# The lower part of w_out's rounded weights: half of it made on GpSimd in two of every four steps

## The chip, the core and the metric
The kernel runs on one core of one Trainium2 chip. The metric is the device time of one execution in microseconds, as the median of several runs. The core has five engines that matter here: TensorE (PE, with its weight loads shown as PEld), VectorE (DVE), ScalarE (ACT), GpSimd (POOL) and SyncE (SP), which issues the transfers.

## The reference
The kernel computes a linear attention with decay and feeds the result to a two-layer network.

```
for each block b of 64 positions:
    intra = (q_b k_b^T * decay mask) v_b
    inter = (q_b * lam^(pos+1)) kv_state
    out[b] = intra + inter
    kv_state = lam^64 * kv_state + (k_b * lam^(63-pos))^T v_b
x = out as 3072 tokens x 512 features
h = x @ w_in                  # 512 x 2048
y = relu(h)^2 @ w_out         # 2048 x 512
```

Everything is float32. There are 4 batches, 8 heads, 768 positions and 64 features in a head.

## The kernel before
**Tokens and slices.** The 3072 tokens make 24 chunks of 128. Four chunks are one slice of 512 tokens, so there are six slices. In a slice the network runs over 16 blocks `f` of 128 hidden features. For each block, `hidden(m, f)` makes h with 12 matmuls, ScalarE and VectorE make relu(h)^2, and `project(m, f)` adds its product with w_out to four PSUM banks (`acc`) with 12 matmuls. The diff touches slice 1 alone, which the code calls m = 0.

**Two parts to each number.** A float32 value is kept as an upper part of few bits and a lower part that holds what is left. A product is the sum of upper times upper, lower times upper and upper times lower. For the weights these parts are `wh` and `wl`: 32 pieces of 128x512 each. In `hidden` the first four matmuls use `wh`, the next four `wl`, the last four `wh` again with the lower part of x (line 581). In `project`, line 617 uses `wh`, line 618 `wl` and line 622 `wh`.

**Units of weights.** The weights come as raw 64-bit numbers and are turned into the two parts while slice 1 runs. This goes by units: unit `u` is a pair of pieces, first the w_in piece of block `u`, then the w_out piece of block `u - 1` (the first and the last unit hold one piece). So a unit is 128x1024, its first 512 columns are due at `hidden(u)` and its last 512 at `project(u - 1)`, which TensorE does just after `hidden(u)`. A unit passes through these steps, each in order:
- `first(u)`, ScalarE, lines 208 and 213: the absolute value of the high words goes to a work tile `A`, and the low words are scaled in place.
- `clamp`, `shift`, `sign`, VectorE, lines 221, 225 and 232: bounds, a shift and the sign, all in `A`.
- `rounded(u)`, VectorE, line 238: adds the low words to `A`. After it the unit's raw buffer is free, and the transfer of unit u + 3 is issued.
- `upper(u)`, ScalarE, line 244: `wh` from `A`.
- `lower(u)`, VectorE, line 247: `wl` = `A` - `wh`, 128x1024 at once.

The pool has two tiles `A`. Unit u + 1 takes the one that unit u - 1 gives back when its last reader is done, so line 208 for u + 1 can't begin before `lower(u - 1)` has ended.

**The order of work in a step.** No scheduler reorders anything: each engine takes its instructions in the order in which the program writes them. Step `f` of slice 1 (with `step = f % 4`, `u_ = f + 2`) writes: `hidden(f)`; on step 2 the attention result of chunk `t`; on step 1 `masked(t)` and `advance(t, 0)` on VectorE (lines 467, 298); `clamp`, `shift` and `sign` of unit f + 2; `upper` and `lower` of unit f + 1; `turn(f + 1)`; on step 1 `fade(t, 1)` (ScalarE, line 508) and `advance(t, 1)` (VectorE, line 298); `rounded(f + 2)`; on step 0 `prep_q` and on step 3 `prep_k`, both on GpSimd (lines 456 and 461); `positive`, `square` (ScalarE, lines 588, 592, 597) and `rest` (VectorE, line 602); on step 2 `attend` (ScalarE 562, VectorE 563); `first(f + 3)` on ScalarE; `project(f - 1)`; on step 0 `look(t)` and `fade(t, 0)`.

**turn.** GpSimd's `turn(u)` (line 254) copies one element of `wl` that `lower(u)` has just written. It makes GpSimd's queue wait for `lower(u)`. Behind it stand `prep_q` or `prep_k`, on steps 0 and 3; on steps 1 and 2 nothing stands behind it but the next step's `turn`.

Of the kernel before, what the change touches and what calls it, by code (L numbers as in the profile page):

```python
# [7 lines left out]
F32 = mybir.dt.float32  # L8
# [4 lines left out]
ALU = mybir.AluOpType  # L13
# [9 lines left out]
DM = H * D  # L23
# [19 lines left out]
def body(ctx: ExitStack, tc: tile.TileContext, qT, kT, kvq, lam, w, out):  # L43
    nc = tc.nc
# [8 lines left out]
    V = nc.vector  # L53
# [19 lines left out]
    def two_banks(pool, name):  # L73
        return pool.tile([P, 2, DM], F32, name=name)
# [62 lines left out]
    def load(t):  # L137
        place(t)
        load_all(t)
        load_kf(t)  # L140
# [29 lines left out]
    wh = const.tile([P, 2 * NF, DM], F32R, name="wh")  # L170
    wl = const.tile([P, 2 * NF, DM], F32R, name="wl")
# [7 lines left out]
    def pieces(u):  # L179
        return slice(max(2 * u - 1, 0), min(2 * u + 1, 2 * NF))  # L180

    raw, cv, hole = {}, {}, None
# [57 lines left out]
    def flat(t, u):  # L240
        return t[:, pieces(u)].rearrange("p a b -> p (a b)")
# [1 line left out]
    def upper(u):  # L243
        nc.scalar.copy(flat(wh, u), cv[u][2].bitcast(F32))

    def lower(u):
        V.tensor_tensor(  # L247
            out=flat(wl, u), in0=cv.pop(u)[2].bitcast(F32), in1=flat(wh, u).bitcast(F32),
            op=ALU.subtract,
        )  # L250


    def turn(u):
        nc.gpsimd.tensor_copy(mark[:, 0:1], wl[0:1, pieces(u).start, 0:1].bitcast(F32))
# [19 lines left out]
    x = ZP  # L274
# [12 lines left out]
    for k in range(4):  # L287
# [10 lines left out]
        lambda o, x, y, op=op: V.tensor_tensor(out=o, in0=x, in1=y, op=op)  # L298
# [5 lines left out]
    b_, t_, u_, c_, d_, af = (sq[:, i, 0 : NS - 1] for i in range(6))  # L304
# [9 lines left out]
    for k in range(1, NS - 1):  # L314
        V.scalar_tensor_tensor(
            out=c_[:, k : k + 1], in0=c_[:, k - 1 : k], scalar=d_[:, k : k + 1],
            in1=c_[:, k : k + 1], op0=ALU.mult, op1=ALU.add,
        )
    add(tr[:, 1:NS], hi_, c_)
    for k in range(NS - 1):  # L320
        n = 1 << k
        x = (tr if k else s)[:, k : k + 1]
        V.tensor_scalar(
            out=pz[:, Z + n : Z + 2 * n], in0=pz[:, Z : Z + n], scalar1=x, scalar2=None, op0=ALU.mult
# [18 lines left out]
    def get_mask():  # L343
# [13 lines left out]
        out=blk, in0=pz[:, Z + 1 : Z + 1 + L].unsqueeze(1).broadcast_to([H, NPR, L]),  # L357
        in1=mine.unsqueeze(2).broadcast_to([H, NPR, L]), op=ALU.mult,
    )
    nc.gpsimd.tensor_tensor(  # L360
        out=four, in0=four, in1=pz[:, Z + L : Z + L + 1].broadcast_to([H, 4]), op=ALU.mult
# [28 lines left out]
    def of(x):  # L390
        return [x[:, k] for k in range(2)]
# [129 lines left out]
    def result(t, banks, begun=(), keys=range(2)):  # L521
        g = Group(banks, begun, keys)
        m, c = a_of.pop(t), chunk.pop(t)

        def value(y, b, a, j):
            if y == 1 - b:
                return c["v"][rows[y], 2 * y + a, j]
            return c["vx"][rows[y], a, j]

        def query(y, b, a, j):  # L530
            x = c["qs"][rows[y], 2 * y + a] if j == y else c["qx"][rows[y], a]
            return x[:, b * L : (b + 1) * L]

        for b in (1, 0):
            old = b or t % NCB
            for a in range(2):
                for y in range(2):
                    for j in range(2):
                        g.put(
                            y, j, (2 * a + b) * L, value(y, b, a, j), m[rows[y], j, b, a],  # L540
                            stop=not old,
                        )
        for b in (0, 1) if t % NCB else (1,):
            s_ = before_block(2 * t + b)
            for a in range(2):
                for y in range(2):
                    for j in range(2):
                        g.put(
                            y, j, (2 * a + b) * L, s_[rows[y], a, j], query(y, b, a, j),
                        )  # L550
        return g.begun
# [22 lines left out]
    def hidden(m, f, xh, xl):  # L574
        h = ps_h.tile([P, N], F32, name="h")
        for _ in range({1: 10, 2: 6}.get(f, 0) if m == 0 else 0):
            nc.tensor.matmul(h, wh[:, 0, 0:P], xh[:, 0], start=True, stop=True)
        k = 0
        for wt, x in ((wh, xh), (wl, xh), (wh, xl)):
            for kt in range(KT):  # L580
                nc.tensor.matmul(  # L581
                    h, wt[:, w_in(f), kt * P : (kt + 1) * P], x[:, kt], start=k == 0, stop=k == 11
                )
                k += 1
        return h

    def positive(h):
        nc.scalar.activation(h, h, AF.Relu)  # L588
# [207 lines left out]
    def new_x(m):  # L796
        xs_of[m] = [wk.tile([P, KT, N], F32R, name=n, tag=n) for n in ("xh", "xl")]
# [96 lines left out]
    for m in range(PLAIN):  # L894
        if m == 0:
            new_x(1)
        else:
            middle.close()
            ps_b = ctx.enter_context(tc.tile_pool(name="ps_b", bufs=1, side="right", space=PSUM))
            held += [  # L900
                wk.tile([P, KT, N], F32, name=f"held{k}", tag=n) for k, n in enumerate(("xh", "xl"))
            ]
        for f in range(NF):
            h = hidden(m, f, *xs_of[m])
            if m == 0:
                t = G + f // 4
                step = f % 4
                u_ = f + 2
                if step == 2:
                    o = two_banks(ps_a, "att")  # L910
                    result(t, of(o))
                    if t + 1 < 2 * G:
                        load(t + 1)
                        load_vx(t + 1)
                    else:
                        for n in (t + 1, t + 2):
                            load_kq(n)
                            load_v(n)
                if step == 1:
                    masked(t)  # L920
                    advance(t, 0)
                if u_ < NLOT:
                    if f:
                        clamp(u_)
                    if f == 1:
                        upper(u_ - 1)
                        lower(u_ - 1)
                    if f:
                        shift(u_)
                    sign(u_)  # L930
                if f > 1:
                    upper(u_ - 1)
                    lower(u_ - 1)
                if f:
                    turn(u_ - 1)
                if step == 1:
                    fade(t, 1)
                    advance(t, 1)
                if f == 0:
                    positive(h)  # L940
                    gh = square(h)
                    rest(m, f, h, gh)
                if u_ < NLOT:
                    rounded(u_)
                    wload(u_ + 3)
                if step == 0 and f:
                    prep_q(t)
                if step == 3 and t + 1 < 2 * G:
                    prep_k(t + 1)
                if f:  # L950
                    positive(h)
                    gh = square(h)
                    rest(m, f, h, gh)
                if step == 1:
                    copy_qx(t)
                if step == 2:
                    attend(t, o)
                if u_ + 1 < NLOT:
                    first(u_ + 1)
                if prev is not None:  # L960
                    project(*prev)
                if step == 0:
                    look(t)
                    fade(t, 0)
            else:
                t = 2 * G + f
                if f == 0:
                    prep_k(t)
                if f <= 2 * G:
                    x = burst(t, f > 0, True, lambda: positive(h))  # L970
                    rest(m, f, h, square(h))
                else:
                    squared(m, f, h)
                if 1 <= f <= 2 * G:
                    keep(t - 1, x)
                if f <= 2 * G:
                    masked(t)
                    state(t)
                    if f:
                        load_v(t + 1)  # L980
                    prep_q(t)
                    if t + 2 < SOLO:
                        load_kq(t + 2)
                    prep_k(t + 1)
                    copy_vx(t)
                if f - 1 in SUMS:
                    w_parts(SUMS.index(f - 1), S)
                if f in SUMS:
                    S = w_sums(SUMS.index(f))
                if f <= 2 * G:  # L990
                    copy_qx(t)
                if f == 2 * G + 1:
                    fetch(0)
                    fetch(1)
                if f > 2 * G:
                    x_sums(f - 2 * G - 1)
                    x_parts(f - 2 * G - 1)
                project(*prev)
            prev = (m, f)
# [104 lines left out]
```

## Time and profile before

| | |
|---|---|
| median of 3 runs | 586.49 us (585.92 to 587.32) |
| the profiled execution, its own time | 586.32 us |
| its span in the trace | 584.6 us |
| TensorE matmul busy | 574.1 us, 98% of the span |
| VectorE busy | 318.7 us, 55% |
| ScalarE busy | 315.2 us, 54% |
| GpSimd busy | 73.2 us, 13% |
| mean granted clock of TensorE | 0.994 of full speed |

Slice 1 runs from 26.4 us on and ends at about 130 us. The busy shares are means over the whole span: in slices of a fortieth, VectorE stands at eight or nine tenths or more nearly all the way to 120 us, and at two to five tenths later on.

### The profile page before, as it was taken

The numbers are of one execution on the slowest core, as the hardware profiler recorded it, in microseconds if no ns is written. First come the engines' busy times: TensorE is split into PE (matmuls) and PEld (weight loads), VectorE is DVE, ScalarE is ACT, GpSimd is POOL, SyncE is SP. The second block draws the span as 40 slices with busy tenths as digits, with TensorE's granted clock in tenths as the row PEclk, the third lists the DMA queues.
The fourth block names the chain that finished last, engine by engine and source line by source line (L and its number), as shares of the span: only waits on it lengthen the run. The fifth ranks groups of instructions, "written<-read, shape, count | busy, mean of one in ns | idle before, by whom it ended". The sixth has DMA issues, their size and how long they took to land.

```text
span 584.6 us, 12762 instructions
## 1 busy us (share of the span) xinstructions
PE 574.1 (98%) x5240; PEld 469.8 (80%) x5240; DVE 318.7 (55%) x586; ACT 315.2 (54%) x578; POOL 73.2 (13%) x87
## 2 busy tenths in 40 slices
PE   8799999999999999999999999999999999999997
PEld 5677788788888888888888888888888888888885
DVE  6899999946868676533444333446433333334222
ACT  3698889845656555445645444634344444444221
POOL 7402230321323100011111101000000000000000
PEclk8899999999999999999999999999999999999999
DMA  8668567146897933856554563300354444411001
GB/s 330 220 219 268 180 227 269 59 145 200 290 374 250 360 140 108 276 168 185 180 166 143 163 182 93 123 1 0 113 157 127 126 125 120 121 50 73 1 0 72
DMA packets 51273, 93.62 MB, mean 160 GB/s; under 512 B 4624, under 2 KB 19472, under 8 KB 51216
## 3 DMA queue, kind: packets, MB, share of 16 engines
q1 hardware_dynamic: 51216, 92.82, 49.2%
q8 instruction: 41, 0.67, 0.5%
q14 instruction: 16, 0.13, 0.1%
HBM read 71.83 MB, written 20.97 MB: 159 GB/s over the span
## 4 chain that ended last, share of the span: by engine, by line
PE 91%; DVE 4%; ACT 3%; issue 1%; DMA 1%; POOL 0%; DVEq 0%; ACTq 0%; POOLq 0%
PE h L723 26%; PE acc L617 15%; PE acc L622 14%; PE acc L618 14%; PE h L581 12%; PE h L384 4%; PE b L384 2%; PE att L79 1%; PE att L384 1%; DVE A L232 1%; PE open L384 1%; DVE A L238 1%; ACT A L208 1%; DMA raw<-in_w 1%; ACT faded L508 0%
## 5 line engine op out<-in xcount | busy, mean ns | idle before, releaser
L617 PE MATMUL acc<-wh,gh 128*128 128x512 f32 x384 | 151.7, 395 | 0.0
L618 PE MATMUL acc<-wl,gh 128*128 128x512 f32 x384 | 149.6, 390 | 0.0
L622 PE MATMUL acc<-wh,gl 128*128 128x512 f32 x384 | 149.3, 390 | 0.0
L617 PEld LDWEIGHTS acc<-wh,gh 128*128 128x128 f32 x384 | 72.1, 188 | 15.8
L622 PEld LDWEIGHTS acc<-wh,gl 128*128 128x128 f32 x384 | 72.1, 188 | 15.1
L618 PEld LDWEIGHTS acc<-wl,gh 128*128 128x128 f32 x384 | 72.1, 188 | 14.5
L602 DVE TENSOR_TENSOR gl<-h,gh 128x512 fp32r<-128x512 f32 x48 | 33.1, 690 | 70.8 <-ACT h L597 70.8
L588 ACT ACTIVATE h<-h 128x512 f32<-128x512 f32 x48 | 28.0, 584 | 72.5 <-PE h L581 38.8
L298 DVE TENSOR_TENSOR temp<-h,temp 128x512 f32<-128x512 f32 x48 | 33.0, 688 | 56.8 <-PE h L723 46.9
L723 PE MATMUL h<-wh,ring 128*128 128x512 f32 x224 | 60.0, 390 | 0.0
L588 ACT ACTIVATE temp<-temp 128x512 f32<-128x512 f32 x16 | 10.1, 632 | 88.6 <-DVE temp L298 88.6
L723 PEld LDWEIGHTS h<-wh,ring 128*128 128x128 f32 x224 | 42.0, 188 | 9.1 <-DVE r L298 0.4
L456 POOL TENSOR_TENSOR qs<-set,qpow 128x512 f32<-128x512 f32 (+1 forms) x21 | 27.0, 1284 | 167.9 <-PE b L384 156.8
L581 PE MATMUL h<-xh,wl 128*128 128x512 f32 x128 | 34.9, 394 | 1.4 <-DVE wl L247 1.2
L298 DVE TENSOR_TENSOR r<-h,temp 128x512 f32<-128x512 f32 x24 | 16.6, 692 | 34.5 <-PE h L723 33.2
L581 PE MATMUL h<-xh,wh 128*128 128x512 f32 x128 | 34.7, 393 | 0.7 <-ACT xh L562 0.7
L723 PE MATMUL h<-wl,ring 128*128 128x512 f32 x112 | 34.5, 389 | 0.0
L602 DVE TENSOR_TENSOR gl<-r,gh 128x512 fp32r<-128x512 f32 x24 | 16.6, 690 | 32.9 <-ACT gh L755 32.9
L581 PE MATMUL h<-xl,wh 128*128 128x512 f32 x128 | 34.2, 389 | 0.0
L755 ACT CAST gh<-r 128x512 fp32r<-128x512 f32 x24 | 14.9, 621 | 30.0 <-PE acc L618 30.0
L581 PEld LDWEIGHTS h<-xh,wl 128*128 128x128 f32 x128 | 23.6, 188 | 8.2 <-DVE wl L247 3.5
L723 PE MATMUL h<-wh 128*128 128x512 f32 x112 | 30.1, 390 | 0.0
(175 smaller groups left out, 1023.6 us busy)
## 6 DMA issues: line engine op xcount, KB each, us to landing
ring<-wd SPq DMA_DIRECT2D x56, 256.0 KB, 2.9
raw<-in_w SPq DMA_DIRECT2D x22, 512.0 KB, 4.8
set<-in_kvq SPq DMA_DIRECT2D x16, 512.0 KB, 4.0
wd<-hl SPq DMA_DIRECT2D x16, 512.0 KB, 5.5
wh<-wd SPq DMA_DIRECT2D x28, 256.0 KB, 2.8
wl<-wd SPq DMA_DIRECT2D x28, 256.0 KB, 2.8
set<-in_kT SPq DMA_DIRECT2D x22, 256.0 KB, 5.1
set<-in_w SPq DMA_DIRECT2D x10, 512.0 KB, 5.8
```

What stands on the lines that cost most here:

```text
L79: nc.tensor.matmul(w_[:, 0], st[:, 0, 0].rearrange("p a b -> p (a b)"), st[:, 0:2].rearrange("p n c a b -> p (n c a b)"), start=True, stop ...
L298: lambda o, x, y, op=op: V.tensor_tensor(out=o, in0=x, in1=y, op=op)
L384: nc.tensor.matmul(self.banks[row][rows[col], at : at + D], lhsT, rhs, start=key not in self.begun, stop=stop, skip_group_check=True,)
L456: nc.gpsimd.tensor_tensor(out=z, in0=x, in1=w_, op=ALU.mult)
L581: nc.tensor.matmul(h, wt[:, w_in(f), kt * P : (kt + 1) * P], x[:, kt], start=k == 0, stop=k == 11)
L588: nc.scalar.activation(h, h, AF.Relu)
L602: V.tensor_tensor(out=gl, in0=r, in1=gh.bitcast(F32), op=ALU.subtract)
L617: nc.tensor.matmul(accs[m][i], gh[:, cs], wh[:, j], start=f == 0, stop=False)
L618: nc.tensor.matmul(accs[m][i], gh[:, cs], wl[:, j], start=False, stop=False)
L622: nc.tensor.matmul(accs[m][i], gl[:, cs], wh[:, j], start=False, stop=end)
L723: nc.tensor.matmul(bank, w[:, kw * HALF + kt * P : kw * HALF + (kt + 1) * P], x_slot(2 * c + kt, kx), start=first and q == 0, stop=q == 5, ...
L755: nc.scalar.copy(gh, r_of[f])
```

## The change
In steps 1 and 2 of four (f = 2, 5, 6, 9, 10, 13, 14), `lower` is split. VectorE subtracts only the first 512 columns, the w_in piece. Then `turn` is written, and behind it GpSimd subtracts the other 512 columns, the w_out piece. In steps 0 and 3 (and f = 1) all stays as it was. The number of turns stays at 15, and no transfer is added or removed.

```diff
-    def lower(u):
-        V.tensor_tensor(
-            out=flat(wl, u), in0=cv.pop(u)[2].bitcast(F32), in1=flat(wh, u).bitcast(F32),
-            op=ALU.subtract,
-        )
+    def lower(u, shared=False):
+        x, h, A = flat(wl, u), flat(wh, u).bitcast(F32), cv.pop(u)[2].bitcast(F32)
+        n = DM if shared else x.shape[1]
+        V.tensor_tensor(out=x[:, 0:n], in0=A[:, 0:n], in1=h[:, 0:n], op=ALU.subtract)
+        if shared:
+            turn(u)
+            nc.gpsimd.tensor_tensor(out=x[:, n:], in0=A[:, n:], in1=h[:, n:], op=ALU.subtract)
...
                 if f > 1:
                     upper(u_ - 1)
-                    lower(u_ - 1)
-                if f:
+                    lower(u_ - 1, step in (1, 2))
+                if f == 1 or f and step in (0, 3):
                     turn(u_ - 1)
```

## Rows read from the trace of the kernel before

**Rows 1.** The page: busy time and share of the span of TensorE, and the shares of the chain that ended last by engine.
```profile
PE 574.1 (98%) x5240; PEld 469.8 (80%) x5240; DVE 318.7 (55%) x586; ACT 315.2 (54%) x578; POOL 73.2 (13%) x87
...
PE 91%; DVE 4%; ACT 3%; issue 1%; DMA 1%; POOL 0%; DVEq 0%; ACTq 0%; POOLq 0%
```

**Rows 2.** The waits in the stretch from 25 to 75 us: who waited for whom, us in total, times, the longest.
```profile
POOL mark L254 <- DVE wl L247: 41.0, 6, 15.5
ACT A L208 <- DVE wl L247: 3.8, 5, 1.3
...
PEld h L581 <- DVE wl L247: 3.0, 4, 1.2
...
PE h L581 <- DVE wl L247: 1.2, 3, 0.8
```

**Rows 3.** TensorE's timeline, the four matmuls of `hidden` that use `wl`, for f = 4, 6, 8, 12, 14 and 15: start, duration, instruction, and the idle time before it with who ended it.
```profile
54.09 1.20 PE L581 MATMUL h<-xh,wl 128*128 128x512 f32 x4 [0.31 <-DVE wl L247]
...
67.33 1.20 PE L581 MATMUL h<-xh,wl 128*128 128x512 f32 x4 [0.77 <-DVE wl L247]
...
79.67 1.07 PE L581 MATMUL h<-xh,wl 128*128 128x512 f32 x4
...
103.83 1.07 PE L581 MATMUL h<-xh,wl 128*128 128x512 f32 x4
...
116.23 1.20 PE L581 MATMUL h<-xh,wl 128*128 128x512 f32 x4
...
123.13 1.07 PE L581 MATMUL h<-xh,wl 128*128 128x512 f32 x4
```

**Rows 4.** VectorE's timeline: step f = 2 from `lower` to the next step's `clamp`, then the same of f = 5 (start, duration, instruction).
```profile
46.76 1.22 DVE L247 TENSOR_TENSOR wl<-A,wh 128x1024 fp32r<-128x1024 f32 x1
47.89 1.22 DVE L238 CUSTOM_DVE_ANT_0 A<-raw,A 128x2048 uint16<-128x2048 uint16 x1
49.03 0.69 DVE L602 TENSOR_TENSOR gl<-h,gh 128x512 fp32r<-128x512 f32 x1
49.63 0.68 DVE L563 TENSOR_TENSOR xl<-att,xh 128x512 fp32r<-128x512 f32 x1
50.22 0.69 DVE L221 TENSOR_SCALAR A<-A 128x1024 f32<-128x1024 f32 x1
...
66.06 1.22 DVE L247 TENSOR_TENSOR wl<-A,wh 128x1024 fp32r<-128x1024 f32 x1
67.20 1.22 DVE L238 CUSTOM_DVE_ANT_0 A<-raw,A 128x2048 uint16<-128x2048 uint16 x1
68.33 0.69 DVE L602 TENSOR_TENSOR gl<-h,gh 128x512 fp32r<-128x512 f32 x1
68.93 0.69 DVE L221 TENSOR_SCALAR A<-A 128x1024 f32<-128x1024 f32 x1
```

**Rows 5.** VectorE's timeline: a `clamp` at f = 4 that lasts longer than the others, `lower` at f = 7, 11, 13, 14 and 15 (the last is half a unit), and, between them, `advance(t, 1)` with the `rounded` behind it at f = 9.
```profile
55.69 1.09 DVE L221 TENSOR_SCALAR A<-A 128x1024 f32<-128x1024 f32 x1
...
77.59 1.22 DVE L247 TENSOR_TENSOR wl<-A,wh 128x1024 fp32r<-128x1024 f32 x1
...
90.98 0.42 DVE L298 TENSOR_TENSOR st<-att,faded 128x256 f32<-128x256 f32 x1
91.32 1.22 DVE L238 CUSTOM_DVE_ANT_0 A<-raw,A 128x2048 uint16<-128x2048 uint16 x1
...
101.70 1.22 DVE L247 TENSOR_TENSOR wl<-A,wh 128x1024 fp32r<-128x1024 f32 x1
...
114.95 1.22 DVE L247 TENSOR_TENSOR wl<-A,wh 128x1024 fp32r<-128x1024 f32 x1
...
119.68 1.22 DVE L247 TENSOR_TENSOR wl<-A,wh 128x1024 fp32r<-128x1024 f32 x1
...
122.62 0.68 DVE L247 TENSOR_TENSOR wl<-A,wh 128x512 fp32r<-128x512 f32 x1
```

**Rows 6.** ScalarE's timeline: the first instruction of `first` at f = 2, 5 and 13 (the last is half a unit), with the idle time before it.
```profile
48.01 1.17 ACT L208 ACTIVATE A<-raw 128x1024 f32<-128x1024 f32 x1 [0.25 <-DVE wl L247]
...
67.31 1.15 ACT L208 ACTIVATE A<-raw 128x1024 f32<-128x1024 f32 x1 [0.81 <-DVE wl L247]
...
116.39 0.68 ACT L208 ACTIVATE A<-raw 128x512 f32<-128x512 f32 x1
```

**Rows 7.** GpSimd's timeline: `turn` at f = 2, `prep_k` behind the turn of f = 3, and `turn` at f = 9 and f = 15.
```profile
48.11 1.04 POOL L254 COPY mark<-wl 1x1 f32<-1x1 f32 x1 [7.20 <-DVE wl L247]
...
55.17 1.05 POOL L461 TENSOR_TENSOR set<-set,near 128x512 f32<-128x512 f32 x1
...
91.20 0.17 POOL L254 COPY mark<-wl 1x1 f32<-1x1 f32 x1 [4.66 <-DVE wl L247]
...
123.43 0.17 POOL L254 COPY mark<-wl 1x1 f32<-1x1 f32 x1 [1.89 <-DVE wl L247]
```

**Rows 8.** GpSimd's groups of instructions by line and shape, over the whole span: count, busy us, mean ns of one, idle before.
```profile
L456 POOL TENSOR_TENSOR qs<-set,qpow 128x512 f32<-128x512 f32 x17 | 23.8, 1402 | 149.7 <-PE b L384 138.7 <-ACT temp L597 11.0
L461 POOL TENSOR_TENSOR set<-set,near 128x512 f32<-128x512 f32 x22 | 23.7, 1075 | 28.1 <-DMA set<-in_kvq 23.6 <-ACT rest L162 3.4 <-ACT near L339 1.0
```

**Rows 9.** Busy time of each engine in two stretches; PEclk is TensorE's granted clock as a share of full speed.
```profile
22.00:24.00 2.00, 0.92 (x60) 0.84 (x52) 1.75 (x3) 1.48 (x4) 1.86 (x2) 1.00 0.02 5
...
123.00:584.00 461.00, 457.54 (x3826) 377.89 (x3824) 207.79 (x408) 218.47 (x418) 37.97 (x33) 1.00 0.46 146
```

## The prediction

> **What bounds the kernel now.** I read the page first. TensorE is busy for 98% of the span and holds 91% of the chain that ended last [rows 1], so whatever makes TensorE wait in slice 1 is added to the end, and whatever ends such a wait is taken off. After 123 us TensorE is busy 457.54 of 461.00 us [rows 9]: nothing there takes a delay back. So the question is only where slice 1 makes TensorE wait, and by how much that moves.
>
> Next I read the waits between 25 and 75 us. The matmuls of `hidden` wait for line 247, `lower`, and for nothing else of VectorE [rows 2]. TensorE's timeline places this: 0.31 us at f = 4 and 0.77 us at f = 6 [rows 3]. Later `lower` keeps a lead. At f = 8 it ends at 77.59 + 1.22 = 78.81 [rows 5], and its matmuls start at 79.67 [rows 3]. With a handover of 0.03 us that lead is 0.83. At f = 12 it is 103.83 - 102.92 - 0.03 = 0.88. At f = 14 it is 116.23 - 116.17 - 0.03 = 0.03, and at f = 15 it is 123.13 - 120.90 - 0.03 = 2.20. (The handover: `lower` at 66.06 ends at 67.28 [rows 4], and ScalarE starts on it at 67.31 [rows 6].) VectorE therefore leads TensorE by almost nothing at f = 4, 6 and 14, and by less than 0.9 us between.
>
> Then VectorE's own timeline. The rows of a step follow each other without a gap [rows 4]; VectorE is full. In the waits, `lower` also holds up ScalarE: line 208 of the next unit waits for it five times in this stretch [rows 2], because the tile `A` that it writes is the one `lower` still reads. This second wait is where the change acts.
>
> **The change part by part.**
>
> *VectorE's half.* One `lower` takes 1.13 us from its start to the next start (46.76 to 47.89, [rows 4]). A half lasts 0.68 us [rows 5], and instructions of that size start 0.60 apart (49.03 to 49.63, [rows 4]). That is 0.53 us less, in seven steps. The w_in piece is ready earlier by as much; at f = 6, where TensorE waited 0.77 us, this is worth up to 0.53 us.
>
> *The turn.* It stays, at the same place behind VectorE's part. At f = 2 it starts 0.13 us after `lower` ends (48.11 against 47.98) and lasts 1.04 us, until 49.15; `rounded` ran until 49.11 [rows 4, 7]. With VectorE idle (f = 15) or busy with `advance` (f = 9) the same copy takes 0.17 us [rows 7]. So GpSimd is kept out of SBUF while `rounded` runs, and gets in 0.04 us after it ends. The reverse shows at f = 4: `prep_k` runs from 55.17 to 56.22 [rows 7], and the `clamp` that starts at 55.69 takes 1.09 instead of 0.69 us [rows 4, 5].
>
> *GpSimd's half.* No row shows a subtraction on GpSimd. The nearest is `prep_k`, 128x512 from two SBUF operands, in 1.05 us [rows 7], 1.075 on average [rows 8]. I take 1.05. Below it could be VectorE's own 0.68; less is excluded, since no GpSimd row of two 128x512 operands is near even that. Above it is the mean of `prep_q`, 1.40 [rows 8], whose second operand is a tile too, where `prep_k` reads one value for each head. On TensorE's side this half costs little, since `project` comes a whole `hidden` later.
>
> The GPSIMD Engine Reference of the Trainium skill (section 3.1) gives 4497 ns for a two-input operation of 2048 columns. Scaled to 512 columns, my estimate from that page is 1.12 us, and by it the sum below would be 4.25 us instead of 3.9.
>
> *The wait that is added.* `A` is now given back when GpSimd has read it, not VectorE. Line 208 of the next unit waits for that; behind it on ScalarE stand line 213, the next `upper` and the squares, and VectorE's next `clamp` waits for line 208. From the start of VectorE's half to the next `clamp`: 0.60 to `rounded`, 1.22 until it ends, 0.04 for the turn, 1.05 for GpSimd's half, 0.03 handover, 1.15 for line 208 [rows 6], 0.03 handover: 4.12 us. Before, it was 68.93 - 66.06 = 2.87 us on step 1, where `rounded` and `rest` fill the time, and 50.22 - 46.76 = 3.46 us on step 2, where `attend` lies between as well [rows 4]. So a shared step on step 1 makes VectorE later by 1.25 us, and one on step 2 by 0.66 us, although each takes 0.53 us off its work. The `rest` and `attend` of that step are not late: the loss is an empty VectorE ahead of the next `clamp`.
>
> *The sum.* VectorE's lateness grows by 0.66 (f = 2), 1.25 and 0.66 (5 and 6), 1.25 and 0.66 (9 and 10): 0.66, then 2.57, then 4.48. Less the lead at each place, TensorE is late by
> - f = 4: 0.66, since it waited there already;
> - f = 6: 0.66 - 0.53 = 0.13, for this unit's own half comes early;
> - f = 8: 2.57 - 0.83 = 1.74;
> - f = 12: 4.48 - 0.88 = 3.60;
> - f = 14: 4.48 - 0.53 - 0.03 = 3.92, its own half early again;
> - f = 15: 4.48 + 1.25 - 0.47 - 0.53 - 2.20 = 2.53 (0.47 because the last line 208 is half as long, [rows 6]).
>
> The lateness that stays is the largest, +3.9 us. Steps 13 and 14 add nothing, since no further full unit waits. Five shared steps count, so each 0.1 us of GpSimd's half is 0.5 us of the end.
>
> *What costs nothing.* No transfer moves ahead of another; weight transfers are issued behind `rounded` and shift with it, as do the GpSimd preparations of steps 0 and 3, whose place behind the turn is unchanged. TensorE's new pauses, up to 1.7 us, get no price for its clock: from 22 to 24 us TensorE was busy 0.92 of 2.00 us with the granted clock at 1.00 [rows 9], the 2.4 GHz level.
>
> The profiled execution took 586.32 us (span 584.6), which is 0.17 below the median. On its own time the sum is 590.2; on the median 586.49 + 3.9 = 590.4.
>
> **The rivals.**
>
> *A, GpSimd's half does not wait for `rounded`: no change or a gain.* The place is the port in the 1.14 us of `rounded`. If a large operation shares it where the one-element copy did not, the half ends 0.68 + 0.13 + 0.17 + 1.05 = 2.03 us after VectorE's half starts, and the next `clamp` can start at 2.03 + 0.03 + 1.15 + 0.03 = 3.24. That is +0.37 on step 1 and -0.22 on step 2; up to f = 14 it is -0.22 + 0.15 + 0.15 - 0.53 = -0.45: 586.0. With a half of 0.68 us nothing would wait for it, and the gain is bounded by TensorE's waits at f = 4 and 6, 0.31 + 0.77 = 1.1, with some tenths more from weight loads [rows 2]: about 585.2. It decides when the half ends less than 2.87 - 1.21 = 1.66 us after VectorE's half starts on step 1, and 2.25 us on step 2. For it: VectorE is full, and its work shrinks by 3.7 us. Against it: the turn's 1.04 against 0.17 us [rows 7], and the 1.09 us `clamp` [rows 5]. Chance 0.13, of which 0.05 beyond 0.2%.
>
> The Trainium skill, Perfetto Trace Analysis, section Optimizing Scalar/DVE Operations, says that moving work from a saturated VectorE to GpSimd may make sense, and adds that the two share a port, so that it might not help. By its first half this rival wins; the rows just named speak for its second.
>
> *B, GpSimd's half gets in ahead of `rounded` on step 1.* At f = 9 `advance` lies between, and the turn ends at 91.37 while `rounded` starts at 91.32 [rows 5, 7]: 0.05 us decide. If GpSimd is first, `rounded` waits; the next `clamp` comes after 2.03 + 1.14 + 0.60 = 3.77 us, where it was 2.87 + 0.34 = 3.21 before: +0.56 instead of +1.25. The sum falls to 3.2: 589.7. Chance 0.2.
>
> *C, GpSimd's half is slow.* With 1.40 us each, five steps add 1.75: 592.2. For it: both operands are full tiles. Against it: `prep_q` reads in a more broken pattern. Chance 0.17.
>
> **How the numbers follow.** The forecast has 0.5 and gives 590.4. The ends of GpSimd's half give 590.4 - 1.85 = 588.5 and 592.1, which also hold B and nearly C; left out are A and a little of C, under 2 in 10. A measurement of this kernel can tell about 0.2%, 1.2 us, from no change. Slower by more than that: forecast, B and C, 0.87. Within: 0.08. Faster: 0.05.
>
> **What would show it.** Right: line 208 at f = 2, 5, 6, 9, 10 waits for GpSimd's new subtraction, some 2 us or more on step 1; VectorE stands idle 1 to 2 us ahead of the `clamp` of f = 3, 6, 7, 10, 11; the new subtractions start where `rounded` ends and last about 1.05 us; TensorE's longest waits in slice 1 are for line 247 at f = 4, 8 and 12, over 1 us each; after 130 us the two traces run alike. Wrong: the subtractions lie beside `rounded`; or line 208 waits no longer than before; or VectorE has no gaps ahead of `clamp`; or TensorE's waits come off at f = 6 and don't return at f = 8.

## The result and the profile after

The median is 591.27 us (590.12 to 592.71) against 586.49 us before (585.92 to 587.32), five runs of each. The ratio is 1.0072, with a 95% interval from 1.0051 to 1.0092: 4.2 us slower, 3.0 to 5.4; the two medians themselves lie 4.8 us apart. The forecast was 590.4, with ends at 588.5 and 592.1 (592.2 by rival C). The profiled execution took 590.12 us, its span 588.3: 3.7 us more than the span before.

The page of the changed kernel, busy times and the chain that ended last by engine (compare [rows 1]):
```profile
PE 574.6 (98%) x5240; PEld 468.9 (80%) x5240; DVE 318.5 (54%) x586; ACT 314.9 (54%) x578; POOL 81.3 (14%) x94
...
PE 81%; DVE 10%; ACT 4%; issue 2%; POOL 2%; DMA 1%; SPq 0%; ACTq 0%; POOLq 0%; DVEq 0%
```
TensorE has the same 5240 matmuls as before. Its share of the chain went from 91% to 81%, VectorE's from 4% to 10%, and GpSimd, which had none, has 2%: more of the chain now runs through VectorE and through what VectorE waits for.

**One measure for all kernels.** The opening, ahead of the steps that the diff touches, does not take the same time in each execution: the `clamp` of step f = 2 starts at 44.17 us in the trace before, at 43.98 in the trace after, and anywhere from 43.93 to 46.22 in those of the experiments. So I read slice 1 as a stretch, from the start of that `clamp` to the start of the `wl` matmuls of `hidden(15)`. Before, it goes from the row below to 123.13 [rows 3]: 78.96 us.
```profile
44.17 0.69 DVE L221 TENSOR_SCALAR A<-A 128x1024 f32<-128x1024 f32 x1
```

VectorE's timeline after: the same `clamp`, then `lower` to the next `clamp` at f = 2, at f = 5 and at f = 9 (compare [rows 4, 5]):
```profile
43.98 0.68 DVE L221 TENSOR_SCALAR A<-A 128x1024 f32<-128x1024 f32 x1
...
46.57 0.69 DVE L249 TENSOR_TENSOR wl<-A,wh 128x512 fp32r<-128x512 f32 x1
47.17 1.22 DVE L238 CUSTOM_DVE_ANT_0 A<-raw,A 128x2048 uint16<-128x2048 uint16 x1
48.31 0.69 DVE L604 TENSOR_TENSOR gl<-h,gh 128x512 fp32r<-128x512 f32 x1
48.91 0.68 DVE L565 TENSOR_TENSOR xl<-att,xh 128x512 fp32r<-128x512 f32 x1
50.86 0.69 DVE L221 TENSOR_SCALAR A<-A 128x1024 f32<-128x1024 f32 x1 [1.27 <-ACT A L208]
...
66.70 0.68 DVE L249 TENSOR_TENSOR wl<-A,wh 128x512 fp32r<-128x512 f32 x1
67.30 1.22 DVE L238 CUSTOM_DVE_ANT_0 A<-raw,A 128x2048 uint16<-128x2048 uint16 x1
68.44 0.68 DVE L604 TENSOR_TENSOR gl<-h,gh 128x512 fp32r<-128x512 f32 x1
71.02 0.69 DVE L221 TENSOR_SCALAR A<-A 128x1024 f32<-128x1024 f32 x1 [1.90 <-ACT A L208]
...
92.76 0.68 DVE L249 TENSOR_TENSOR wl<-A,wh 128x512 fp32r<-128x512 f32 x1
93.36 0.42 DVE L300 TENSOR_TENSOR st<-att,faded 128x256 f32<-128x256 f32 x1
93.70 2.38 DVE L238 CUSTOM_DVE_ANT_0 A<-raw,A 128x2048 uint16<-128x2048 uint16 x1
96.01 0.68 DVE L604 TENSOR_TENSOR gl<-h,gh 128x512 fp32r<-128x512 f32 x1
96.61 0.68 DVE L221 TENSOR_SCALAR A<-A 128x1024 f32<-128x1024 f32 x1
```
The reader is to see three things. VectorE's part now lasts 0.69 instead of 1.22 us. At f = 2 and 5 `rounded`, `rest` and `attend` follow it as closely as before, and then VectorE stands empty for 1.27 and 1.90 us ahead of the next `clamp`, waiting for line 208. At f = 9 there is no such hole, but `rounded` lasts 2.38 us instead of 1.22.

ScalarE's timeline after: line 208 at f = 2, 5 and 9 (compare [rows 6]), with the idle time before it:
```profile
49.70 1.12 ACT L208 ACTIVATE A<-raw 128x1024 f32<-128x1024 f32 x1 [2.16 <-POOL wl L252]
...
69.83 1.15 ACT L208 ACTIVATE A<-raw 128x1024 f32<-128x1024 f32 x1 [2.69 <-POOL wl L252]
...
95.03 1.16 ACT L208 ACTIVATE A<-set 128x1024 f32<-128x1024 f32 x1 [1.06 <-POOL wl L252]
```
GpSimd's timeline after: its half at f = 2 and 5, then the turn and the half of f = 9 (compare [rows 7]):
```profile
48.39 1.28 POOL L252 TENSOR_TENSOR wl<-A,wh 128x512 fp32r<-128x512 f32 x1
...
68.52 1.28 POOL L252 TENSOR_TENSOR wl<-A,wh 128x512 fp32r<-128x512 f32 x1
...
93.58 0.17 POOL L256 COPY mark<-wl 1x1 f32<-1x1 f32 x1 [4.12 <-DVE wl L249]
93.72 1.28 POOL L252 TENSOR_TENSOR wl<-A,wh 128x512 fp32r<-128x512 f32 x1
```
Line 208 waits for GpSimd now: 2.16 us where it was 0.25, and 2.69 where it was 0.81. The half starts when `rounded` ends (47.17 + 1.22 = 48.39) and takes 1.28 us; line 208 starts 0.03 us after it.

TensorE's timeline after: the first four matmuls of `hidden` at f = 4, and the `wl` matmuls at f = 4, 6, 8, 12, 14 and 15 (compare [rows 3]):
```profile
52.86 1.20 PE L583 MATMUL h<-xh,wh 128*128 128x512 f32 x4 [0.32 <-ACT wh L244]
54.73 1.19 PE L583 MATMUL h<-xh,wl 128*128 128x512 f32 x4 [0.68 <-DVE wl L249]
...
67.44 1.20 PE L583 MATMUL h<-xh,wl 128*128 128x512 f32 x4 [0.22 <-DVE wl L249]
...
81.78 1.21 PE L583 MATMUL h<-xh,wl 128*128 128x512 f32 x4 [0.67 <-DVE wl L249]
...
107.36 1.20 PE L583 MATMUL h<-xh,wl 128*128 128x512 f32 x4 [0.69 <-DVE wl L249]
...
120.03 1.20 PE L583 MATMUL h<-xh,wl 128*128 128x512 f32 x4 [0.17 <-DVE wl L249]
...
126.93 1.07 PE L583 MATMUL h<-xh,wl 128*128 128x512 f32 x4
```
From 43.98 to 126.93 are 82.95 us, 3.99 us more than before. The wait at f = 6 shrank from 0.77 to 0.22 us, the one at f = 4 grew, and f = 8, 12 and 14 have waits that were not there. After f = 15 nothing is given back: the `wl` matmuls of the first block of slice 2 start 5.44 us later in both traces (132.37 and 128.57).

### The profile page after: what moved, and what is told of

It reads as the page before. It is cut to its first block, busy times and chain, and to the rows that moved or that the text cites. A ratio compares the mean times of both kernels' runs of the same rounds, so it can differ in the third digit from the quotient of the medians.

```text
span 588.3 us, 12767 instructions
## 1 busy us (share of the span) xinstructions
PE 574.6 (98%) x5240; PEld 468.9 (80%) x5240; DVE 318.5 (54%) x586; ACT 314.9 (54%) x578; POOL 81.3 (14%) x94
## 4 chain that ended last, share of the span: by engine, by line
PE 81%; DVE 10%; ACT 4%; issue 2%; POOL 2%; DMA 1%; SPq 0%; ACTq 0%; POOLq 0%; DVEq 0%
PE h L725 26%; PE acc L619 13%; PE acc L624 13%; PE acc L620 13%; PE h L583 8%; PE h L386 4%; DVE A L232 3%; PE b L386 2%; ACT A L208 2%; DVE A L221 2%; DVE A L225 1%; DVE A L238 1%; DVE wl L249 1%; POOL wl L252 1%; DMA raw<-in_w 1%
```

## The experiments

Two theories stood against each other. **The late tile:** the loss comes from `A`, which is given back when GpSimd has read it; line 208 and VectorE's next `clamp` wait for that. **The port:** VectorE and GpSimd lose time to each other in SBUF, whichever tile they read. (SBUF is the memory in which these tiles lie; "the port" names here only what the runs show, that one of the two engines waits there until the other's instruction is done.)

| kernel | median, us | ratio to before (95% interval) | stretch against before, us |
|---|---|---|---|
| the changed kernel | 591.27 | 1.0072 (1.0051 to 1.0092) | +3.99 |
| 1: A released early | 585.5 | 0.9974 (0.9964 to 0.9984) | -1.35 |
| 2: VectorE alone | 587.66 | 1.0018 (1.0008 to 1.0027) | +1.58 |
| 3: no turn | 589.67 | 1.0050 (1.0035 to 1.0066) | +3.19 |
| 4: the half twice | 600.03 | 1.0227 (1.0203 to 1.0251) | +11.61 |
| 5: step 2 only | 589.28 | 1.0057 (1.0045 to 1.0069) | +2.44 |
| 6: step 1 only | 588.88 | 1.0040 (1.0028 to 1.0052) | +1.51 |
| 7: a tile of its own | 586.16 | 0.9988 (0.9976 to 1.0000) | -0.78 |
| 8: rest first | 586.79 | 1.0004 (0.9993 to 1.0014) | +0.04 |

The kernel before, run beside them, had a median of 586.85 us with 1 to 4 and of 586.73 us with 5 to 8. The last column is the stretch defined above, from each kernel's profiled execution, less 78.96 us.

### 1. A released early

```diff
-            nc.gpsimd.tensor_tensor(out=x[:, n:], in0=A[:, n:], in1=h[:, n:], op=ALU.subtract)
+            nc.gpsimd.tensor_tensor(out=x[:, n:], in0=h[:, n:], in1=h[:, n:], op=ALU.subtract)
```
Expected: 

> The changed kernel, but GpSimd's half reads wh in place of A as its first operand (so these columns of wl hold zeros: that part of the computation is left out). Same instruction, same size, same place and port use; only A is given back as soon as VectorE's half is done. Theory (the late A is the loss): line 208 waits no longer than before, the empty VectorE ahead of clamp is gone, TensorE's waits at f = 8 and 12 are gone, and VectorE's saving of 0.53 us in each shared step shows: 1.0 to 1.5 us under the kernel before, 585.0 to 585.5. Rival (GpSimd and VectorE lose time to each other at the port): the loss stays, about +3.8 us over the kernel before, 590.3.

Measured: 585.5 us, 1.5 us (0.9 to 2.1) under before. GpSimd's timeline, the half at f = 2, and TensorE's, the `wl` matmuls of f = 15:
```profile
50.03 1.03 POOL L252 TENSOR_TENSOR wl<-wh 128x512 fp32r<-128x512 f32 x1
```
```profile
123.23 1.07 PE L583 MATMUL h<-xh,wl 128*128 128x512 f32 x4
```
The stretch, from a `clamp` at 45.62, is 77.61 us. GpSimd runs an instruction of the same size in the same place, and TensorE's loss is gone; what shows is VectorE's saving. The port's part is still there. VectorE's `clamp` behind f = 5 and its `rounded` at f = 9:
```profile
69.31 1.07 DVE L221 TENSOR_SCALAR A<-A 128x1024 f32<-128x1024 f32 x1
...
91.01 2.13 DVE L238 CUSTOM_DVE_ANT_0 A<-raw,A 128x2048 uint16<-128x2048 uint16 x1
```
GpSimd holds them up, to 1.07 instead of 0.69 us and 2.13 instead of 1.22, so VectorE gains less than 0.53 us at f = 5 and loses 0.4 at f = 9; what the other steps save is more than that. One thing is not equal: with one tile as both operands the half takes 1.03 us, not 1.28. A quarter of a microsecond in five steps is 1.2 us, and the two kernels are 5.3 us apart in the stretch; so the late tile stands, and the port as the main cause falls.

### 2. VectorE alone

```diff
         if shared:
-            turn(u)
-            nc.gpsimd.tensor_tensor(out=x[:, n:], in0=A[:, n:], in1=h[:, n:], op=ALU.subtract)
+            second.append((u, lambda: V.tensor_tensor(out=x[:, n:], in0=A[:, n:], in1=h[:, n:], op=ALU.subtract)))
...
                     rounded(u_)
+                    for u, half in second:
+                        half()
+                        turn(u)
+                    second.clear()
```
`second` is a list that is empty at the start.

Expected: 

> The same seven steps, but the second half of lower is made by VectorE, right behind rounded; GpSimd has no part in it. VectorE has 0.07 us more work in each of these steps, and A is given back 0.60 + 1.14 + 0.68 = 2.42 us after lower starts instead of 1.22. Theory (the late A): the next clamp comes 3.63 us after lower starts where it was 2.87 (step 1) and 3.46 (step 2), so +0.76 and +0.17; up to f = 14, five steps and its own early half: 0.17 + 0.93 + 0.93 - 0.53 = +1.5 us, 588.0. Rival (the port): no GpSimd, so no loss beyond 0.4 us of work, and 0.53 us earlier w_in pieces: 586.0 to 586.9.

Measured: 587.66 us, by the ratio 1.1 us over before (0.5 to 1.6), and 1.58 us in the stretch. VectorE's timeline at f = 5, the late half (line 253), `rest` and the next `clamp`:
```profile
68.97 0.68 DVE L253 TENSOR_TENSOR wl<-A,wh 128x512 fp32r<-128x512 f32 x1
69.57 0.69 DVE L605 TENSOR_TENSOR gl<-h,gh 128x512 fp32r<-128x512 f32 x1
70.88 0.70 DVE L221 TENSOR_SCALAR A<-A 128x1024 f32<-128x1024 f32 x1 [0.63 <-ACT A L208]
```
Without GpSimd the same hole opens, 0.63 us wide, since line 208 now waits for VectorE's late half. So it is the lateness of the read that costs, not who reads.

### 3. No turn

```diff
         if shared:
-            turn(u)
             nc.gpsimd.tensor_tensor(out=x[:, n:], in0=A[:, n:], in1=h[:, n:], op=ALU.subtract)
```
Expected: 

> The changed kernel without the turn ahead of GpSimd's half, in the seven shared steps: the half now waits only for upper, which ends while VectorE is in sign. If GpSimd can work beside sign (two operands in SBUF), it ends before VectorE's half or just behind it, A is not late, and the time is 1 to 1.5 us under the kernel before: 585.0 to 585.5. If sign and lower keep GpSimd out as rounded does, it gets in behind rounded as with the turn (+3.8 us), or slips in between two instructions and holds the next one up by up to 1.28 us, less the 0.53 saved: five steps of 0.75 us, less the lead, +2.5 to +3.5 us: 589 to 590.

Measured: 589.67 us, +2.9 us. GpSimd's half at f = 2, then VectorE's `lower` at f = 2, `shift` at f = 5 and `sign` at f = 10:
```profile
45.45 2.32 POOL L251 TENSOR_TENSOR wl<-A,wh 128x512 fp32r<-128x512 f32 x1 [4.77 <-ACT wh L244]
```
```profile
46.54 1.78 DVE L249 TENSOR_TENSOR wl<-A,wh 128x512 fp32r<-128x512 f32 x1
...
64.53 1.77 DVE L225 TENSOR_SCALAR A<-A 128x1024 uint32<-128x1024 uint32 x1
...
96.48 2.21 DVE L232 SCALAR_TENSOR_TENSOR A<-set,A 128x1024 uint32<-128x1024 uint32 x1
```
Here `A` is hardly late, and the loss is the port's. The half is issued at 45.45, while `sign` runs from 45.39; it lasts 2.32 us, and VectorE's `lower`, which follows `sign`, takes 1.78 us instead of 0.68. At f = 5 it is `shift` that takes 1.77 us instead of 0.69, at f = 10 `sign` with 2.21 instead of 1.23. Six shared steps up to f = 13 lose 1.1 us each in this way (0.98 at f = 10) and save 0.53: 6.4 - 3.2 = 3.2 us, and the stretch shows 3.19. So the port is a second way to lose nearly as much, and the turn chose between the two.

### 4. The half twice

```diff
             nc.gpsimd.tensor_tensor(out=x[:, n:], in0=A[:, n:], in1=h[:, n:], op=ALU.subtract)
+            nc.gpsimd.tensor_tensor(out=x[:, n:], in0=A[:, n:], in1=h[:, n:], op=ALU.subtract)
```
Expected: 

> The changed kernel with GpSimd's half made twice over (the same instruction again, the same result). Theory: A is late by 1.28 us more in each shared step, five steps count: +6.4 us over the changed kernel less some tenths, 10 to 11 us over the kernel before, 596.5 to 597.5. If the loss were a fixed one per shared step (a handover or a wait for the port, whatever the length), the second instruction would lie in the empty time and cost under 1 us.

Measured: 600.03 us (two runs), more than expected. In the stretch it is 7.6 us over the changed kernel, not 6.4; the matmuls of the first block of slice 2 come another 0.8 us later. VectorE's `clamp` after the step f = 2, with the hole before it, and TensorE where it waits for GpSimd:
```profile
53.39 0.69 DVE L221 TENSOR_SCALAR A<-A 128x1024 f32<-128x1024 f32 x1 [2.63 <-ACT A L208]
```
```profile
110.72 0.50 PE L621 MATMUL acc<-wl,gh 128*128 128x512 f32 x1 [1.41 <-POOL wl L253]
```
The hole grew from 1.27 to 2.63 us, about the 1.35 us from the start of one GpSimd instruction to the start of the next; the theory had 1.28. Two things came on top. At f = 9 the second instruction was shut out by `rounded` and took 2.15 us, and line 208 waited for that as well. And `project` itself waited for the w_out piece, 1.41 us at `project(10)`, which I had left out. A fixed loss per step is ruled out.

### 5 and 6. Each step alone

```diff
-                    lower(u_ - 1, step in (1, 2))
-                if f == 1 or f and step in (0, 3):
+                    lower(u_ - 1, step == 2)             # 5; step == 1 in 6
+                if f == 1 or f and step != 2:            # 5; step != 1 in 6
```
Expected of 5: 

> The split in step 2 alone (f = 2, 6, 10, 14). With the 1.28 us that GpSimd's half takes in the trace of the changed kernel, the next clamp comes 0.60 + 1.22 + 0.04 + 1.28 + 0.03 + 1.15 + 0.03 = 4.35 us after lower starts, where it was 3.46: +0.89 us for each of f = 2, 6, 10, and nothing early at f = 6 and 14, since their units are whole. Theory (late A): 3 times 0.89, less the lead of 0.03 us at f = 14: +2.6 us, 589.4. Rival (the loss belongs to step 1, where GpSimd has no cover by attend): under 0.5 us.

Expected of 6: 

> The split in step 1 alone (f = 5, 9, 13). At f = 5 the next clamp is late by 4.35 - 2.87 = 1.48 us; at f = 9 GpSimd gets in ahead of rounded, which then lasts 2.38 us, so that VectorE is late by 2.38 - 1.22 - 0.53 = 0.6 us. At f = 14 its own half is 0.53 early. Theory (late A): 1.48 + 0.63 - 0.53 = +1.5 us, 588.4; together with the split in step 2 alone this makes the whole of the change. Rival (the loss belongs to step 2): 0.5 us faster than before, by the early halves.

Measured: 589.28 and 588.88 us; in the stretch +2.44 and +1.51, together 3.95, where both at once gave 3.99. VectorE's timeline of 5, the `clamp` after f = 2 and f = 6, and of 6, the `clamp` after f = 5 and `rounded` at f = 9:
```profile
52.76 0.69 DVE L221 TENSOR_SCALAR A<-A 128x1024 f32<-128x1024 f32 x1 [1.28 <-ACT A L208]
...
78.35 0.69 DVE L221 TENSOR_SCALAR A<-A 128x1024 f32<-128x1024 f32 x1 [1.27 <-ACT A L208]
```
```profile
71.92 0.69 DVE L221 TENSOR_SCALAR A<-A 128x1024 f32<-128x1024 f32 x1 [1.90 <-ACT A L208]
...
93.76 2.38 DVE L238 CUSTOM_DVE_ANT_0 A<-raw,A 128x2048 uint16<-128x2048 uint16 x1
```
Each part does on its own what it does in the whole, and neither step can be left as the harmless one: the cover by `attend` on step 2 is 0.60 us, the wait it should hide is longer.

### 7. A tile of its own

```diff
     def rounded(u):
-        V.tensor_tensor(out=A, in0=A, in1=L, op=ALU.add)
+        n = DM if u in apart else A.shape[1]              # apart = (3, 7, 11, 15)
+        V.tensor_tensor(out=A[:, 0:n], in0=A[:, 0:n], in1=L[:, 0:n], op=ALU.add)
+        if u in apart:
+            spare[u] = wk.tile([P, DM], U32, name="spare", tag="a")
+            V.tensor_tensor(out=spare[u], in0=A[:, n:], in1=L[:, n:], op=ALU.add)
```
`upper` reads the two in two instructions, GpSimd's half reads `spare`, and the split is on step 2 alone.

Expected: 

> The split in step 2 alone, and rounded writes the w_out half of these units (3, 7, 11, 15) into a tile of its own, as two instructions of half size; upper reads it in two as well, and GpSimd's half reads that tile. So A comes back when VectorE's half is done, and nothing is left out. Theory (late A): VectorE has 0.53 us less in step 2 and 0.07 more in step 1, ScalarE 0.1 us more; up to 0.2 us a time is lost where GpSimd's 1.28 us reach into the next clamp. Three steps count: 0.2 to 1.2 us under the kernel before, 585.6 to 586.6. If A were not the cause, it would stay at the time of the split in step 2 alone, some 2.5 us over the kernel before.

Measured: 586.16 us, ratio 0.9988 (0.9976 to 1.0000): 0.7 us under before, with no change just at the edge of the interval, and 3.1 us under the split in step 2 alone. VectorE's `clamp` of f = 2 and of f = 3:
```profile
43.93 0.68 DVE L222 TENSOR_SCALAR A<-A 128x1024 f32<-128x1024 f32 x1
...
49.46 0.73 DVE L222 TENSOR_SCALAR A<-A 128x1024 f32<-128x1024 f32 x1
```
ScalarE's `first` at f = 2 (line 208 before, 209 here) and GpSimd's half there:
```profile
47.40 1.18 ACT L209 ACTIVATE A<-raw 128x1024 f32<-128x1024 f32 x1
```
```profile
48.34 1.29 POOL L261 TENSOR_TENSOR wl<-spare,wh 128x512 fp32r<-128x512 f32 x1
```
GpSimd's half is as long as in the changed kernel and still starts behind `rounded`, but line 209 starts before it, without a wait. From `clamp` to `clamp` are 5.53 us, where the kernel before takes 6.05 (44.17 to 50.22) and the split in step 2 alone 6.88. Here the step gets what the change was after. The `clamp` of f = 3 takes 0.73 instead of 0.69 us; that is all it loses there to GpSimd's half. It has the lowest median of these kernels that leave nothing out, though a gain over the kernel before is not shown.

### 8. Rest first

```diff
-                if u_ < NLOT:
+                if u_ < NLOT and step != 2:
                     rounded(u_)
                     wload(u_ + 3)
...
                 if step == 2:
                     attend(t, o)
+                    if u_ < NLOT:
+                        rounded(u_)
+                        wload(u_ + 3)
```
with the split in step 2 alone.

Expected: 

> The split in step 2 alone, with rest and attend written ahead of rounded there, so that GpSimd's half has the port for 1.19 us just behind the turn and A comes back 0.69 + 0.13 + 0.14 + 1.28 = 2.24 us after lower starts instead of 3.14. Then line 208 ends at 2.24 + 0.03 + 1.15 = 3.42 and the next clamp comes at about 3.45, as before (3.46); VectorE's saving is just used up. Theory (late A): no change against the kernel before within 0.5 us, 2 us or more under the split in step 2 alone. Rival (the port, whatever the order): rounded is held up instead and the loss of the split in step 2 alone stays.

Measured: 586.79 us, ratio 1.0004, no change. VectorE's `rounded` and the next `clamp` at f = 2:
```profile
50.61 1.52 DVE L238 CUSTOM_DVE_ANT_0 A<-raw,A 128x2048 uint16<-128x2048 uint16 x1
52.28 0.70 DVE L221 TENSOR_SCALAR A<-A 128x1024 f32<-128x1024 f32 x1 [0.15 <-ACT A L208]
```
GpSimd's half there:
```profile
49.76 1.28 POOL L252 TENSOR_TENSOR wl<-A,wh 128x512 fp32r<-128x512 f32 x1
```
`rounded` is held up until GpSimd is done and takes 1.52 us, and the hole is 0.15 us. `A` comes back earlier than in experiment 5, and what is still lost just uses up VectorE's saving.

## Why the prediction was right, and where it was not

**The step that carries it held.** The forecast was that line 208 would wait for GpSimd's read of `A`, that VectorE's next `clamp` would wait for line 208, and that the lateness at f = 14 would stay until the end. The traces show each link, experiment 1 takes the first away and the loss at the end is gone, and experiment 7 does so, for step 2 alone, with the whole computation kept. The one step that went another way is f = 9 (below). The sum was 3.92 us; the stretch shows 3.99.

**That the sum came out so close is luck: two of its terms erred against each other.** VectorE's lateness by step, `lower` to the next `clamp`, against the same in the trace before:

| step | forecast | measured |
|---|---|---|
| f = 2 | 0.66 | 4.29 - 3.46 = 0.83 |
| f = 5 | 1.25 | 4.32 - 2.87 = 1.45 |
| f = 6 | 0.66 | 4.29 - 3.47 = 0.82 |
| f = 9 | 1.25 | 3.85 - 3.20 = 0.65 |
| f = 10 | 0.66 | 4.29 - 3.47 = 0.82 |
| sum | 4.48 | 4.57 |

The late tile makes 3.92 us of the 4.57 (all steps but f = 9), and the port the 0.65 at f = 9. With the half's true length and no rival B the last column would have 1.45 at f = 9 too, 5.37 in all, and the sum 5.37 - 0.53 - 0.03 = 4.8 us; with B and a half of 1.05 us it would have been 3.2.

*GpSimd's half was taken at 1.05 us and takes 1.28.* All seven do, within 0.01 us:
```profile
L252 POOL TENSOR_TENSOR wl<-A,wh 128x512 fp32r<-128x512 f32 x7 | 9.0, 1284 | 0.0
```
I had taken `prep_k` as the nearest row, though the forecast itself named why `prep_q` was nearer in kind: its second operand is a full tile. And I had read `prep_q` by its mean over the whole span, 1.40 us [rows 8], which mixes rows of 1.3 us with others of 1.5 and more. In slice 1 of the kernel before, next to the change, it took 1.29 and 1.30 us:
```profile
61.04 1.29 POOL L456 TENSOR_TENSOR qs<-set,qpow 128x512 f32<-128x512 f32 x1
```
That row was the price of the half, to 0.01 us. In experiment 1, with one tile as both operands, the half took 1.03 us. The estimate from the Trainium skill, GPSIMD Engine Reference, section 3.1, was 1.12 us; the trace has 1.28, so the Trainium skill's figure, scaled by the columns, comes out too low here as well. The longer half added 0.16 to 0.20 us at each of four steps; of the 0.23, about 0.04 came back since the half starts when `rounded` ends and not 0.04 us later.

*At f = 9 rival B came true.* The turn ended at 93.75 and GpSimd's half started at 93.72, `rounded` at 93.70; GpSimd was served first and `rounded` took 2.38 us. VectorE's next `clamp` follows `rest` without a gap, so the wait for line 208 costs nothing there. The step cost 0.65 us, where B had 0.56 and the forecast 1.25. I gave B 0.2 on its own; it belonged with the forecast, since it happened at f = 9 and f = 13 here and again in experiment 6.

**Rival A is refuted.** GpSimd's half never lay beside `rounded`, and experiment 3 shows that it can't lie beside `sign`, `shift` or `lower` without holding one of them up. The Trainium skill, Perfetto Trace Analysis, Optimizing Scalar/DVE Operations, says that moving work from a saturated VectorE to GpSimd may make sense, and that it might not help because the two share a port. The traces agree with the second half: `rounded` took 2.38 us at f = 9. More was lost by the late tile. **Rival C** had 1.40 us for the half; the measured 1.28 lies nearer to C than to the forecast's 1.05.

**What I had not priced.** The forecast named `upper` behind line 208, but put no wait of TensorE on it. `upper` is late too, and the first matmuls of `hidden` wait for it at f = 4 (0.32 us) and f = 8 (0.35). The `wl` matmuls, for which I had said "over 1 us each", wait 0.68, 0.67 and 0.69 us at f = 4, 8 and 12; only the weight loads in front of them wait over 1 us (1.11, 1.11 and 1.13). `project` was said to cost little: the weight loads of line 620 wait for GpSimd's half at f = 3 and 7, 0.35 and 0.52 us. The sum is not touched, since VectorE's lateness sets it.

**Readings to put right.** The leads at odd f were left out. From f = 5 to 13 they are 1.0 to 1.8 us, not "less than 0.9 us", and being longer they don't set the end. VectorE is not quite full either: at f = 5 and 13 it stands 0.89 and 0.91 us ahead of `advance`, waiting for ScalarE's `fade`; after the change these gaps are 0.89 and 0.86 us, so they took next to nothing of the lateness back. And its busy share from 117 to about 250 us is four to eight tenths in slices of a fortieth, not "two to five"; nothing else rests on that.

**What the saving was worth.** VectorE's 0.53 us in each of seven steps are real. Experiment 1 shows what is left of them when line 208 does not wait and the port still costs something at f = 5 and 9: 1.35 us in the stretch, not 3.7. TensorE had little more than the waits of 0.31 and 0.77 us [rows 3] to give back.

## What to carry to other kernels

Splitting an instruction over two engines makes every tile that it reads come free when the slower of the two is done; look first for who is waiting for that tile, and price the wait from there, not from the work that is saved. If the tile has a waiter, give the second engine a tile of its own before giving it the work. Where the two engines share a port, the second one's work is free only beside instructions of the first that don't need it (here `rest` and `attend`, which read from PSUM), and that cover has to be as long as the work. To price an instruction on another engine, take single rows of the same kind from the stretch that changes, not a mean over the whole span.

## What the runs showed of the hardware

GpSimd's subtraction of 128x512 took 1.28 us from two different tiles and 1.03 us when both operands were the same tile. VectorE and GpSimd held each other off for whole instructions. Hundredths of a microsecond decided which was served first, and the recorded starts don't always tell it: in experiment 3 `sign`, recorded 0.06 us ahead of the half, kept it out at f = 2, and at f = 5 the half, recorded 0.07 us ahead, held up `shift`; but `rounded` took 2.38 us at f = 9 of the changed kernel behind a half recorded as starting 0.02 us after it. On VectorE this held for instructions with one operand in SBUF (`shift`, 1.77 instead of 0.69 us) and with two (`sign`, 2.21 instead of 1.23; the half `lower`, 1.78 instead of 0.68), while `rest` and `attend`, which read one operand from PSUM, kept their 0.69 us beside GpSimd.
